# Windowed attention, forward and backward: one 64x64-mode stretch for four tiles, the last chunk of a projection in two banks, loads on two queues, and a rearranged start and end

## The chip, the cores and the metric

The kernel runs on one core of a Trainium2 chip. The metric is the device time of one execution in microseconds (us). Every kernel was run three times, plus once under the profiler; medians are over these four runs (over three for the 2076.62 us of the kernel before).

## The reference, cut to what matters

The inputs are an image `x` of 256x256 pixels with C = 384 channels, in bfloat16, the weights `wqkv` (384x1152) and `wo` (384x384), and `grad_out`, shaped like `x`. The image is cut into 8x8 windows of 64 tokens, and each window is one attention problem with one head.

```python
qkv = xw @ wqkv                       # xw: windows x 64 tokens x 384
p = softmax(einsum('bqc,bkc->bqk', q, k) * C ** -0.5)
o = einsum('bqk,bkc->bqc', p, v) @ wo
# outputs: o, and the gradients of x, wqkv and wo for grad_out
```

There are 1024 windows. The kernels put two windows on the 128 partitions (a "tile") and handle four tiles (a "quad", n = 0 to 127) in a step.

## The kernel before: the parts that matter

The weights are multiplied with each other once at the start (`A` = the scaled product of the q and k weights, `B` = that of the v weights and `wo`, and both transposes). The loop is a software pipeline: step n finishes quad T = n, does the scores and the softmax of S = n + 1, and the projections of A = n + 2.

PSUM is `PS`, eight banks of 512 float32 a partition. `PB` holds the softmax's probabilities and their gradient, `YHT` the projected x and grad_out (transposed), `YH` the same turned back by a transposing DMA, `TT` the transposed `PB`, `MD` what the output and the gradient of x are made from, and `VW` what the weight gradients are made from. The parts that the change touches:

```python
def load(n):                                     # eight loads, one queue (SyncE, "SP")
    for t in range(4):
        SP.dma_start(out=X[:, (n % NX) * 4 + t, :], in_=img(x, n, t))
        SP.dma_start(out=DO[:, (n % ND) * 4 + t, :], in_=img(grad_out, n, t))

def proj(n, a, banks, engs):                     # three chunks of 512 columns, a bank each
    ...
    for mo in range(CK):
        o = PS[:, banks[mo], :]
        for m in range(CK):
            mm(o.rearrange("p (t k) -> p t k", t=4), wgt[:, m, mo * P:(mo + 1) * P], src[:, m, :, :],
               m == 0, m == CK - 1)
        ev(engs[mo], YHT[:, n % NYH, a, mo, :], o)

# the order of a step (conditions cut)
load(n + 4); turn_in(n + 3)                      # loads; transposing DMAs X -> XT, DO -> DOT
scores(S); chain1(S)                             # 64-column products; the softmax's first part on DVE
md(T)                                            # 64x64 products
wgrad(g, k0)
chain2(S); chain3(S)                             # the rest of the softmax: ACT, DVE, POOL
outs(T, 0, 0, ACT); outs(T, 2, 2, DVE); outs_st(T)
proj(A, 0, (4, 5, 0), (ACT, DVE, ACT)); turn_yh(A, 0)
wgrad(g, k0 + 1)
attn(T, 0, 2, 4); attn_ev(T, 0, 2, DVE)          # first stretch in 64x64 mode: two tiles
attn(T, 1, 0, 5); attn_ev(T, 1, 0, ACT)
dxs(T, 0, 4, ACT); dxs_st(T, 0)
proj(A, 1, (2, 3, 1), (DVE, ACT, DVE)); turn_yh(A, 1)
turn_p(S); turn_p_ev(S)                          # transposes of PB, into TT
attn(T, 2, 2, 4); attn_ev(T, 2, 2, ACT)          # second stretch: two tiles
attn(T, 3, 0, 5); attn_ev(T, 3, 0, DVE)
dxs(T, 2, 4, ACT); dxs_st(T, 2)
```

`wgrad` sums a part of a weight gradient over three quads in bank 7, always that bank, and DVE adds it to `ACC`. The plain loads of the weights come first at the start, then `load(0)`, then the transposes of the weights from on-chip memory, all on SP's queue but for the load of `wo`.

Of the kernel before, what the change touches and what calls it, by code (L numbers as in the profile page):

```python
# [9 lines left out]
ALU = mybir.AluOpType  # L10
# [6 lines left out]
def kernel(  # L17
# [27 lines left out]
    PS = pp.tile([P, 8, 512], F32, name="PS")  # L45
    X = sb.tile([P, NX * 4, C], BF16, name="X")
# [42 lines left out]
    def load(n):  # L89
        for t in range(4):  # L90
            SP.dma_start(out=X[:, (n % NX) * 4 + t, :], in_=img(x, n, t))  # L91
            SP.dma_start(out=DO[:, (n % ND) * 4 + t, :], in_=img(grad_out, n, t))  # L92

    def turn_in(n):
        xs = X[:, (n % NX) * 4:(n % NX) * 4 + 4, :].rearrange("p t c -> p (t c)")
        SP.dma_start_transpose(out=XT[:, n % NXT, :, :], in_=xs)  # L96
        ds = DO[:, (n % ND) * 4:(n % ND) * 4 + 4, :].rearrange("p t c -> p (t c)")
        SP.dma_start_transpose(out=DOT[:, n % NDT, :, :], in_=ds)  # L98
# [5 lines left out]
    def proj(n, a, banks, engs):  # L104
        wgt = A_sb if a == 0 else BT_sb
        src = (XT[:, n % NXT] if a == 0 else DOT[:, n % NDT]).rearrange("p (t m) k -> p m t k", m=CK)
        for mo in range(CK):
            o = PS[:, banks[mo], :]
            for m in range(CK):
                mm(o.rearrange("p (t k) -> p t k", t=4), wgt[:, m, mo * P:(mo + 1) * P], src[:, m, :, :],  # L110
                   m == 0, m == CK - 1)
            ev(engs[mo], YHT[:, n % NYH, a, mo, :], o)
# [18 lines left out]
    def chain2(n):  # L131
        ACT.activation(out=PEX[:], in_=SS[:], func=ACTF.Exp)
# [11 lines left out]
    def turn_p(n):  # L144
        bb = PS[:, 6, :].bitcast(BF16)
        for t in range(4):
            for a in range(2):
                for w in range(2):
                    r = slice(64 * w, 64 * w + 64)
                    PE.transpose(bb[r, t * P + a * 64:t * P + a * 64 + 64], PB[r, n % 2, a, t, :], ident[r, r])  # L150

    def turn_p_ev(n):
        ev(DVE, TT[:, n % 2].rearrange("p t a k -> p (t a k)"), PS[:, 6, :].bitcast(BF16)[:, 0:512])

    def md(n):
        for m in range(CK):
# [22 lines left out]
    def attn(n, t, bvw, bdx):  # L179
        xs, ds, vw = (n % NX) * 4 + t, (n % ND) * 4 + t, (n % NVW) * 4 + t  # L180
        for a in range(2):
            src = X[:, xs, :] if a == 0 else DO[:, ds, :]
            yh = YH[:, n % NTOK, a, :, :].rearrange("p (m t) k -> p t m k", m=CK)[:, t]
            for cr in range(2):
                for w in range(2):
                    r = slice(64 * w, 64 * w + 64)
                    o = 64 * (w if cr == 0 else 1 - w)
                    if cr == 0:
                        mm(PS[o:o + 64, bvw + a, 0:C], PB[r, n % 2, a, t, :], src[r, :], True, True)
                    else:  # L190
                        mm(PS[o:o + 64, bdx, 0:C].rearrange("p (m k) -> p m k", m=CK), PB[r, n % 2, a, t, :],
                           yh[r], a == 0, False)

    def attn_ev(n, t, bvw, eng):
        ev(eng, VW[:, (n % NVW) * 4 + t, :, :], PS[:, bvw:bvw + 2, 0:C])

    def dxs(n, t0, b0, eng):
        for i in range(2):
            for m in range(CK):
                mm(PS[:, b0 + i, 0:C], MD[:, m, t0 + i, 0:2, :].rearrange("p a k -> p (a k)"), AT_sb[:, m, :],  # L200
                   False, m == CK - 1)
        ev(eng, DXS[:, n % 2, t0:t0 + 2, :], PS[:, b0:b0 + 2, 0:C])
# [6 lines left out]
    def wgrad(g, k):  # L209
        quads = range(g * GQ, min(NQ, (g + 1) * GQ))  # L210
        which, ma = k // CK, k % CK
        tiles = [(q, t) for q in quads for t in range(4)]
        for i, (q, t) in enumerate(tiles):
            mm(PS[:, 7, 0:C], X[:, (q % NX) * 4 + t, ma * P:(ma + 1) * P], VW[:, (q % NVW) * 4 + t, which, :],
               i == 0, i == len(tiles) - 1)
        if g == 0:
            DVE.tensor_copy(out=ACC[:, k, :], in_=PS[:, 7, 0:C])
        else:
            DVE.tensor_tensor(out=ACC[:, k, :], in0=PS[:, 7, 0:C], in1=ACC[:, k, :], op=ALU.add)  # L219

    with tc.manual_schedule():

        wT = VW[:].rearrange("p a b c -> p (a b c)")[:, 0:JK * C].rearrange("p (j c) -> p j c", j=JK)
        wo_sb = VW[:].rearrange("p a b c -> p (a b c)")[:, JK * C:(JK + CK) * C].rearrange("p (m c) -> p m c", m=CK)
        for m in range(CK):
            SP.dma_start(out=w_sb[:, m, :], in_=wqkv[m * P:(m + 1) * P, :])
        ACT.dma_start(out=wo_sb[:], in_=wo.rearrange("(m p) n -> p m n", p=P))
        make_identity(nc, ident[:])
        load(0)
        for m in range(CK):  # L230
            SP.dma_start_transpose(out=wT[:, :, m * P:(m + 1) * P], in_=w_sb[:, m, :])  # L231
        for m in range(CK):
            SP.dma_start_transpose(out=woT_sb[:, :, m * P:(m + 1) * P], in_=wo_sb[:, m, :])  # L233
        k = 0
        for dst, lt, r0, sc in ((A_sb, wT[:, 0:CK], wT[:, CK:2 * CK], True),
                                (AT_sb, wT[:, CK:2 * CK], wT[:, 0:CK], True),
                                (B_sb, wT[:, 2 * CK:3 * CK], wo_sb, False),
                                (BT_sb, wo_sb, wT[:, 2 * CK:3 * CK], False)):
            for mo in range(CK):
                o = PS[:, k % 8, 0:C]  # L240
                for m in range(CK):
                    mm(o, lt[:, m, mo * P:(mo + 1) * P], r0[:, m, :], m == 0, m == CK - 1)
                if sc:
                    ACT.activation(out=dst[:, mo, :], in_=o, func=ACTF.Copy, scale=scale)
                else:
                    DVE.tensor_copy(out=dst[:, mo, :], in_=o)
                k += 1

        def step(n):
            T, S, A = n, n + 1, n + 2  # L250
            doT, doS, doA = 0 <= T < NQ, 0 <= S < NQ, 0 <= A < NQ
            g, k0 = n // GQ - 1, 2 * (n % GQ)
            doF = 0 <= g < NG
            if 0 < n + 4 < NQ:
                load(n + 4)
            if 0 <= n + 3 < NQ:
                turn_in(n + 3)
            if doS:
                scores(S)
                chain1(S)  # L260
            if doT:
                md(T)
            if doF:
                wgrad(g, k0)
            if doS:
                chain2(S)
                chain3(S)
            if doT:
                outs(T, 0, 0, ACT)
                outs(T, 2, 2, DVE)  # L270
                outs_st(T)
            if doA:
                proj(A, 0, (4, 5, 0), (ACT, DVE, ACT))
                turn_yh(A, 0)
            if doF:
                wgrad(g, k0 + 1)
            if doT:
                attn(T, 0, 2, 4)
                attn_ev(T, 0, 2, DVE)
                attn(T, 1, 0, 5)  # L280
                attn_ev(T, 1, 0, ACT)
                dxs(T, 0, 4, ACT)
                dxs_st(T, 0)
            if doA:
                proj(A, 1, (2, 3, 1), (DVE, ACT, DVE))
                turn_yh(A, 1)
            if doS:
                turn_p(S)
                turn_p_ev(S)
            if doT:  # L290
                attn(T, 2, 2, 4)
                attn_ev(T, 2, 2, ACT)
                attn(T, 3, 0, 5)
                attn_ev(T, 3, 0, DVE)
                dxs(T, 2, 4, ACT)
                dxs_st(T, 2)

        for n in range(-3, GQ * NG + GQ):
            step(n)


        GF = YHT[:, 0].rearrange("p a m t -> p (a m t)")[:, 0:6 * C].rearrange("p (k c) -> p k c", k=6)
        GFT = YHT[:, 1].rearrange("p a m t -> p (a m t)")[:, 0:6 * C].rearrange("p (k c) -> p k c", k=6)
        for k in range(6):
            ev(DVE if k < 3 else ACT, GF[:, k, :], ACC[:, k, :])
        for h in range(2):
            for mb in range(CK):
# [3 lines left out]
                ev(DVE if h == 0 else ACT, GFT[:, h * CK + mb, :], pt[:, 0:C])  # L311
        dw = VW[:].rearrange("p a b c -> p (a b c)")[:, 0:CK * J].rearrange("p (m j) -> p m j", m=CK)
        dwo = VW[:].rearrange("p a b c -> p (a b c)")[:, CK * J:CK * J + CK * C].rearrange("p (m j) -> p m j", m=CK)
        k = 0
        for ma in range(CK):
            for col, lt, rr, r0 in ((0, GF[:, 0:CK], w_sb, C), (C, GFT[:, 0:CK], w_sb, 0), (2 * C, GFT[:, CK:], woT_sb, 0)):
# [46 lines left out]
```

## Time and profile before

The time before is 2076.62 us (median of three runs, 2074.34 to 2076.63). These lines are from the first, third and fourth parts of its profile page: busy time, share of the span and number of instructions by engine (PE is the matmuls of TensorE, PEld its weight loads); the two large DMA queues with packets, MB and the share of 16 engines' time (q1 is what SyncE issues, q0 what GpSimd issues; ScalarE's few loads are on q10, under 1 MB); and the chain of waits that ended last, by engine.

```profile
PE 2029.9 (98%) x26970; PEld 1149.4 (55%) x26970; DVE 1358.6 (66%) x2452; ACT 985.1 (48%) x1555; POOL 1012.9 (49%) x1798
q1 hardware_dynamic: 956304, 305.37, 84.1%
q0 software_dynamic: 73728, 101.02, 18.2%
PE 96%; DMA 2%; SPq 2%; DVE 0%; ACT 0%; issue 0%; DVEq 0%
```

TensorE is the limit. I take a step as the time from the first score product of one quad to that of the next. The windows view of the kernel before, cut at the scores of quad 1, quad 6 and quad 127, shows the three stages: head, 121 full steps and tail. Columns: stretch, its length, busy us (and instructions) of PE, PEld, DVE, ACT and POOL, the granted clock, the DMA share (the summed time of all packets over that of 16 engines, so it can pass 1), GB/s.

```profile
0.00:42.55 42.55, 21.48 (x137) 9.89 (x138) 10.19 (x20) 8.15 (x14) 2.03 (x8) 0.92 0.81 176
42.55:122.32 79.77, 70.59 (x979) 37.80 (x978) 50.21 (x89) 37.30 (x59) 37.45 (x66) 0.98 1.01 200
122.32:2017.68 1895.36, 1894.67 (x25412) 1076.88 (x25411) 1274.46 (x2299) 921.97 (x1452) 956.70 (x1694) 1.00 1.06 203
2017.68:2072.70 55.02, 43.20 (x447) 24.80 (x446) 23.71 (x44) 17.63 (x30) 16.72 (x30) 0.98 0.24 62
```

In the third line PE is busy 1894.67 of 1895.36 us: a gain there has to come out of PE's own order of work. But "busy" hides short stalls, since the ends of matmuls are modelled. The timeline of the kernel before, at the second attention stretch of one step, shows such a stall (columns: start, duration, engine, line, operation, out<-in, number, and in brackets the idle time before it):

```profile
1013.08 0.69 DVE L79 CAST YHT<-PS 128x512 bf16<-128x512 f32 x1 [0.67 <-PE PS L73]
...
1013.35 0.33 PE L73 MATMUL PS<-DO,PB 64*64 64x384 bf16 x2
1013.45 0.33 PE L73 MATMUL PS<-YH,PB 64*64 64x384 bf16 x2
1013.51 0.33 PE L73 MATMUL PS<-X,PB 64*64 64x384 bf16 x2
...
1013.83 0.35 PE L73 MATMUL PS<-DO,PB 64*64 64x384 bf16 x2
```

Pairs of matmuls on one tile start every 0.16 us (1013.35 to 1013.51), but the next pair starts 0.32 us later, at 1013.83. DVE's eviction of the projection's last chunk, which holds bank 1, ended at 1013.77; the stalled products write bank 1. The stall is 0.155 us by the unrounded starts, in every step.

Waits of PE outside the steady state, from the waits view of the kernel before (us in total, times, longest):

```profile
PE PS L73 <- DMA VW<-w_sb: 14.0, 1, 14.0
PE PS L73 <- DMA XT<-X: 10.2, 5, 3.5
PE PS L73 <- DVE ACC L219: 4.5, 7, 0.6
```

They are the start (the transposed weights), the first steps (the transposed x) and the end (bank 7 shared by the last weight gradients).

### The profile page before, as it was taken

To read this page: it belongs to the slowest core of one execution; us is meant where nothing else is said; L and a number is where in the kernel's file an instruction comes from. 1 tells how busy PE (TensorE), PEld (TensorE's weight loads), DVE (VectorE), ACT (ScalarE), POOL (GpSimd) and SP (SyncE) were. 2 spreads that over 40 slices of the span, in tenths; PEclk is the share of its full clock that TensorE was granted. 3 is DMA by queue.
4 is the path that set the end of the run, shared out by engine and by line. 5 is a ranking of instruction groups with operands and counts; after the bars stand their busy time and mean duration, and the time that the engine had idled before them with its cause. 6 is when DMAs were issued, how large, how long until landed. Compare 5 with 4: busy or idle time off the path is not lost.

```text
span 2072.7 us, 65934 instructions
## 1 busy us (share of the span) xinstructions
PE 2029.9 (98%) x26970; PEld 1149.4 (55%) x26970; DVE 1358.6 (66%) x2452; ACT 985.1 (48%) x1555; POOL 1012.9 (49%) x1798
## 2 busy tenths in 40 slices
PE   5899999999999999999999999999999999999997
PEld 2455555555555555555555555555555555555554
DVE  3566666666666666666666666666666666666664
ACT  2444444444445444444444444544444444444452
POOL 1454555555555455455555555545545555555552
PEclk9999999999999999999999999999999999999999
DMA  8999999999999999999999999999999999999991
GB/s 177 203 202 202 208 201 197 209 205 198 205 207 200 204 206 200 202 209 198 206 200 205 203 204 203 202 203 205 200 201 208 202 201 204 206 204 200 206 177 56
DMA packets 1030734, 410.90 MB, mean 198 GB/s; under 512 B 865056, under 2 KB 1013280, under 8 KB 1030432
## 3 DMA queue, kind: packets, MB, share of 16 engines
q1 hardware_dynamic: 956304, 305.37, 84.1%
q0 software_dynamic: 73728, 101.02, 18.2%
q8 instruction: 212, 3.47, 0.7%
q14 instruction: 90, 0.74, 0.1%
q10 hardware_dynamic: 400, 0.29, 0.0%
HBM read 101.84 MB, written 101.84 MB: 98 GB/s over the span
## 4 chain that ended last, share of the span: by engine, by line
PE 96%; DMA 2%; SPq 2%; DVE 0%; ACT 0%; issue 0%; DVEq 0%
PE PS L73 94%; PE PS L150 2%; DMA XT<-X 1%; SPq L92 0%; SPq L91 0%; SPq L231 0%; DMA VW<-in_wo_dram 0%; DVE ACC L219 0%; SPq L233 0%; ACT DXS L77 0%; ACT YHT L77 0%; SPq L98 0%; DVE YHT L79 0%; SPq L96 0%; PE PS L310 0%
## 5 line engine op out<-in xcount | busy, mean ns | idle before, releaser
L207 POOL DMA_DIRECT2D out_dram<-DXS x1024 | 572.8, 566 | 583.7 <-ACT DXS L77 561.4
L73 PE MATMUL PS<-VW,X 128*128 128x384 bf16 x3072 | 542.7, 326 | 4.5 <-DVE ACC L219 4.5
L73 PEld LDWEIGHTS <-X 64*64 64x64 bf16 (+1 forms) x9216 | 380.3, 104 | 218.8 <-issue 6.9
L79 DVE CAST YHT<-PS 128x512 bf16<-128x512 f32 x384 | 264.3, 688 | 240.4 <-PE PS L73 238.4
L73 PEld LDWEIGHTS <-MD 128*128 128x128 bf16 x3072 | 279.3, 98 | 232.4 <-issue 61.5
L77 ACT CAST VW<-PS 128x768 bf16<-128x768 f32 x256 | 204.3, 798 | 367.6 <-PE PS L73 367.6
L77 ACT CAST YHT<-PS 128x512 bf16<-128x512 f32 x384 | 224.7, 585 | 277.6 <-PE PS L73 253.7
L219 DVE TENSOR_TENSOR ACC<-PS,ACC 128x384 f32<-128x384 f32 x252 | 140.5, 558 | 257.3 <-PE PS L73 257.3
L73 PE MATMUL PS<-AT_sb,MD 128*128 128x384 bf16 x1536 | 294.1, 328 | 0.0
L141 POOL TENSOR_TENSOR UM<-PB,ST 128x256 f32<-128x256 bf16 x128 | 77.8, 608 | 424.1 <-PE PS L73 367.8
L73 PE MATMUL PS<-XT,A_sb 128*128 128x512 bf16 x1152 | 273.7, 383 | 10.4 <-DMA XT<-X 10.2
L177 POOL DMA_DIRECT2D out_dram<-OS x512 | 276.1, 545 | 13.9 <-issue 11.4
L73 PE MATMUL PS<-B_sb,MD 128*128 128x384 bf16 x1536 | 271.5, 326 | 4.3 <-DVE MD L79 2.5
L73 PE MATMUL PS<-DOT,BT_sb 128*128 128x512 bf16 x1152 | 270.5, 380 | 0.0
L77 ACT CAST DXS<-PS 128x768 bf16<-128x768 f32 x256 | 204.3, 798 | 138.3 <-PE PS L73 138.3
L79 DVE CAST VW<-PS 128x768 bf16<-128x768 f32 x256 | 244.0, 953 | 18.6 <-PE PS L73 4.8
L79 DVE CAST MD<-PS 128x512 bf16<-128x512 f32 x384 | 240.2, 681 | 0.6 <-PE PS L73 0.6
L73 PE MATMUL PS<-YH,PB 64*64 64x384 bf16 x2048 | 238.6, 332 | 1.0 <-ACT DXS L77 1.0
L77 ACT CAST MD<-PS 128x512 bf16<-128x512 f32 x384 | 200.1, 594 | 67.1 <-DVE ST L128 64.6
L77 ACT CAST OS<-PS 128x768 bf16<-128x768 f32 x128 | 102.1, 798 | 194.5 <-PE PS L73 194.5
L73 PEld LDWEIGHTS <-A_sb 128*128 128x128 bf16 x1152 | 113.4, 99 | 135.6 <-issue 12.4
L73 PEld LDWEIGHTS <-BT_sb 128*128 128x128 bf16 x1152 | 113.1, 98 | 123.8 <-issue 2.4
(46 smaller groups left out, 1618.6 us busy)
## 6 DMA issues: line engine op xcount, KB each, us to landing
X<-in_x_dram SPq DMA_DIRECT2D x512, 96.0 KB, 3.1
DO<-in_grad_out_dram SPq DMA_DIRECT2D x512, 96.0 KB, 3.2
out_dram<-OS POOLq DMA_DIRECT2D x512, 96.0 KB, 2.9
out_dram<-DXS POOLq DMA_DIRECT2D x1024, 48.0 KB, 3.8
YH<-YHT SPq DMA_TRANSPOSE x256, 5.4
XT<-X SPq DMA_TRANSPOSE x128, 6.6
DOT<-DO SPq DMA_TRANSPOSE x128, 6.5
w_sb<-in_wqkv_dram SPq DMA_DIRECT2D x3, 288.0 KB, 4.0
```

The lines of the kernel that those rows point to most:

```text
L73: PE.matmul(out, lhsT=lhsT, rhs=rhs, start=start, stop=stop, skip_group_check=True)
L77: ACT.copy(out=out, in_=in_)
L79: DVE.tensor_copy(out=out, in_=in_)
L141: POOL.tensor_tensor(out=UM[:], in0=pb[:, 1], in1=bcast(3), op=ALU.mult)
L150: PE.transpose(bb[r, t * P + a * 64:t * P + a * 64 + 64], PB[r, n % 2, a, t, :], ident[r, r])
L177: POOL.dma_start(out=img(out_0, n, t), in_=OS[:, n % 2, t, :])
L207: POOL.dma_start(out=img(out_1, n, t)[8 * w:8 * w + 8], in_=DXS[64 * (1 - w):64 * (1 - w) + 64, n % 2, t, :])
L219: DVE.tensor_tensor(out=ACC[:, k, :], in0=PS[:, 7, 0:C], in1=ACC[:, k, :], op=ALU.add)
```

## The change

Its intent, as I read the diff: (1) the four attention products of a step stand together, so that the engine enters and leaves the 64x64 mode once where it did twice; PSUM is addressed flat, and products that cross a bank are cut at its edge; the softmax's first part moves behind `md`. (2) The last chunk of each projection goes to two banks in halves, so that two engines evict it in halves. (3) The loads of x move from SP's queue to POOL's. (4) At the start, the weights are transposed straight from memory, the loads are spread over three queues and held back by small POOL copies ("gates"), and the first projections start earlier. (5) At the end, the last eight weight gradients use five banks, and the last products are reordered.

```diff
-    def load(n):
+    def load_x(q, n):
         for t in range(4):
-            SP.dma_start(out=X[:, (n % NX) * 4 + t, :], in_=img(x, n, t))
-            SP.dma_start(out=DO[:, (n % ND) * 4 + t, :], in_=img(grad_out, n, t))
+            q.dma_start(out=X[:, (n % NX) * 4 + t, :], in_=img(x, n, t))
+    def load_do(q, n):                            # the same for grad_out
 ... in proj:
-            o = PS[:, banks[mo], :]
+            for t0, t1 in ((0, 4),) if mo < CK - 1 else ((0, 2), (2, 4)):
+                o = PS[:, banks[i], 0:P * (t1 - t0)]
 ... 
+    def attn_all(n, S):
+        v = (n % NVW) * 4
+        fvw = ((3072, 3584), (1536, 1920), (2304, 2688), (3072, 3584))   # columns; a bank has 512
+        for t in range(4):
+            attn(n, t, 0, fvw[t][0], t * C)
+            if t == 2:
+                ev(ACT, VW[:, v + 1, :, :].rearrange("p a c -> p (a c)"), PSF[:, 1536:2304])
+            attn(n, t, 1, fvw[t][1], t * C)
+            if t == 0:
+                ev(ACT, VW[:, v, 0, :], PSF[:, 3072:3456])
+                ev(DVE, VW[:, v, 1, :], PSF[:, 3584:3968])
+        ev(DVE, VW[:, v + 2, :, :].rearrange("p a c -> p (a c)"), PSF[:, 2304:3072])
+        if S is not None:
+            turn_p(S)
+        ev(ACT, VW[:, v + 3, 0, :], PSF[:, 3072:3456])
+        ev(DVE, VW[:, v + 3, 1, :], PSF[:, 3584:3968])
+        if S is not None:
+            turn_p_ev(S)
 ... the new order of a step (conditions cut)
+        load_do(SP, n + 4); load_x(POOL, n + 4); turn_in(n + 3, 0); turn_in(n + 3, 1)
+        scores(S); md(T); chain1(S)
+        wgrad(g, k0)
+        chain2(S); chain3(S)
+        outs(T, 0, 0, ACT); outs(T, 2, 2, DVE); outs_st(T)
+        wgrad(g, k0 + 1)
+        proj(A, 0, (3, 1, 2, 5), (ACT, DVE, ACT, DVE)); turn_yh(A, 0)
+        attn_all(T, S if doS else None)
+        dxs(T, 0); dxs_ev(T, 0, ACT)
+        proj(A, 1, (3, 4, 5, 7), (ACT, DVE, ACT, DVE)); turn_yh(A, 1)
+        dxs(T, 1); dxs_ev(T, 1, ACT)
 ... the start (cut)
         for m in range(CK):
-            SP.dma_start(out=w_sb[:, m, :], in_=wqkv[m * P:(m + 1) * P, :])
+            SP.dma_start_transpose(out=wT[:, 0:2 * CK, m * P:(m + 1) * P], in_=wqkv[m * P:(m + 1) * P, 0:2 * C])
+        load_x(ACT, 0)
+        load_do(POOL, 0)
+        for i in range(14):
+            mm(PS[:, 7, :], wsrc[:, 0:P], wsrc, True, True)
+        wprod(A_sb, wT[:, 0:CK], wT[:, CK:2 * CK], True)
+        gate(A_sb[0:1, 2, 0:1])                   # a POOL copy: POOL's later loads wait for it
 ... the end (cut)
+        for n in range(NQ, GQ * NG + GQ):
+            for i in range(2):
+                wgrad(n // GQ - 1, 2 * (n % GQ) + i, (3, 4, 5, 6, 7)[b % 5])
+                b += 1
```

## The prediction

> **What bounds it now.** TensorE. The page's first part has PE busy 98%; the windows view has it busy 156.60 of 156.60 us anywhere in the middle; the chain of waits is 96% PE. The timeline shows equal steps (four 8x8-window tiles each): score products start every 15.66 us. DVE 66%, ACT 48%, POOL 49% are not the limit.
>
> One step, by PE starts in the timeline: scores 0.88, md 0.79, weight gradient 1.96, outs 1.95, projection 1.95, weight gradient 2.04, attention of two tiles 0.78, dx 0.98, projection 2.04, transposes and attention of two tiles 1.21, dx 1.08 us. Four 64x64 matmuls already run side by side (one group of four per 0.163 us), so the attention products alone need 1.30 us.
>
> **What changes in a step.**
> - Merging two 64x64 stretches removes two changes of tile mode. The Trainium skill, "TensorEngine Tiling (Array Packing)", Key Properties, says that a change of mode drains the engine; the trace agrees: a projection or attention group followed by another mode is 0.09 to 0.13 us longer. Gain about 0.21 us.
> - The second stretch stalls 0.155 us before the last tile, waiting for DVE's 0.69 us eviction of the projection's last chunk. Two half evictions and later use remove it.
> - Split matmuls cost little: 128-column transposes follow each other every 0.056 us, so a cut adds about 3 ns; about 16 cuts on the critical path, 0.06 us.
> - New: the softmax's first part now stands behind DVE's three MD evictions (0.63 us each). By my sum DVE ends the output eviction of bank 3 about 7.7 us into the step; the projection that now starts with bank 3 is ready at 7.53. I expect a stall of 0 to 0.25 us there.
>
> Net 0.08 to 0.28 us a step; I take 0.17, times 121 full steps: 20 us.
>
> **Head.** Before, the first five steps take 11.7, 14.3, 15.6, 18.2 and 16.1 us, though three of them lack weight gradients (about 11.6 us of PE work); PE waits there for the XT transposes (waits view), and the SP queue issues without a pause: eight loads of about 0.64 us and four transposes of 2.1 to 2.6 us. Moving x loads to POOL takes 2.5 us a step from SP; transposing weights straight from memory shortens the start. Scores of step 0 should move from 42.6 to about 27 us, and step 5 from 122.3 to about 100: 20 us (12 to 28).
>
> **Tail.** The last eight weight gradients share one bank: six 0.65 us waits for DVE in the timeline, and more elsewhere. Five banks remove them: about 5 us. No separate cast of the gradients, fewer stalls in the last step, reordered outputs: about 4 us. In all 9 us.
>
> **Off the path.** POOL gets four more DMA issues a step (0.56 us each): about 10.3 of 15.5 us, still ahead of the transposes of P. DMA bytes do not change. In steady state SP is already ahead of PE, so its relief buys nothing there.
>
> **Sum:** 2076.6 - 20 - 20 - 9 = about 2027 us. Range 1998 to 2050. Chances: faster by over 2% 0.66, within 2% 0.32, slower 0.02.
>
> **What would show it.** Timeline: step period 15.4 to 15.58; one attention stretch near 1.3 us followed without a gap by the transposes; PE waits for the DVE output eviction before the first projection, if my stall is real; scores of step 0 near 27 us; tail from the last step's end to the span's end about 23 us, before 31.
>
> **What would make it wrong.** Bank conflicts between attention groups and evictions in the tightly packed banks (t=3 needs banks 6 and 7 about 0.1 us after they come free); POOL's late x loads delaying XT; SWDGE loads slowing the transposes; head loads serialized by the gates.

## The result, and the profile after

The kernel after is correct. Its time is 2020.70 us (median of four runs, 2020.39 to 2021.47), beside 2076.62 us of before. The ratio is 0.9734, with a 95% interval of 0.9717 to 0.9751. Ratios here are those of the runs of the two kernels in the same rounds, so not quite the ratio of the medians that I quote.

The page of the kernel after, the same parts as before:

```profile
PE 1987.0 (98%) x30568; PEld 1321.4 (65%) x30568; DVE 1392.1 (69%) x2705; ACT 1014.3 (50%) x1810; POOL 1287.7 (64%) x2312
q1 hardware_dynamic: 882128, 254.31, 78.2%
q0 software_dynamic: 98304, 151.39, 28.7%
PE 95%; DMA 2%; issue 1%; SPq 1%; ACT 0%; DVE 0%; POOL 0%; ACTq 0%; POOLq 0%; DVEq 0%
```

The limit is still TensorE, and some 50 MB of loads have moved from q1 to q0. The windows view of the kernel after, cut at the same events (scores of quads 1, 6 and 127):

```profile
0.00:37.02 37.02, 24.58 (x162) 12.06 (x163) 10.72 (x23) 8.55 (x17) 12.95 (x30) 0.86 0.90 167
37.02:113.52 76.50, 67.06 (x1119) 45.01 (x1119) 50.38 (x99) 38.16 (x69) 45.41 (x82) 0.98 1.17 214
113.52:1970.89 1857.37, 1853.89 (x28800) 1238.08 (x28800) 1308.39 (x2541) 950.46 (x1694) 1212.07 (x2171) 1.00 1.10 207
1970.89:2019.69 48.80, 41.51 (x491) 26.24 (x490) 22.64 (x42) 17.16 (x30) 17.25 (x31) 1.00 0.29 73
```

Subtracting stage by stage gives where the 53.0 us between the two profiled spans came from:

| stage | before | after | gain | predicted |
|---|---|---|---|---|
| head, to the scores of quad 6 ("step 5") | 122.32 | 113.52 | 8.8 | 20 |
| 121 full steps | 1895.36 (15.664 each) | 1857.37 (15.350 each) | 38.0 | 20 |
| tail, from the last scores | 55.02 | 48.80 | 6.2 | 9 |

The sum came out as predicted to within 4 us (49 against 53.0), but from other parts: the steady steps gave twice what I had expected, the head less than half.

The median step fell from 15.658 to 15.311 us, below the 15.4 to 15.58 that the prediction names. (The mean of after, 15.350, is higher because of six slow steps, up to 16.89 us.) The pieces of one step, measured between the starts of their first matmuls (us; a piece that ends in a stall or in a change of mode holds it):

| piece | before | after |
|---|---|---|
| scores, md | 0.88 + 0.80 | 0.88 + 0.80 |
| two weight gradients | 1.961 + 2.044 | 1.961 + 1.966 |
| outs | 1.950 | 1.950 |
| two projections | 1.942 + 2.036 | 2.041 + 1.950 |
| attention and the transposes of PB | 0.776 + 1.209 | 1.334 + 0.366 |
| dx, two halves | 0.986 + 1.078 | 0.993 + 1.076 |

A 128x128 group that is followed by attention is 0.08 to 0.09 us longer (2.044 against 1.961, 2.041 against 1.950). Before there were two such groups in a step, after there is one. The attention and transposes together fell from 1.985 to 1.700 us.

The timeline of the kernel after around the first projection and the attention. The bank-3 wait that I had predicted shows in its first two lines: DVE's eviction ends at 12.40 and the projection starts at 12.45.

```profile
1011.45 0.95 DVE L80 CAST OS<-PS 128x768 bf16<-128x768 f32 x1
1012.45 2.11 PE L74 MATMUL PS<-XT,A_sb 128*128 128x512 bf16 x12
...
1014.49 0.35 PE L74 MATMUL PS<-X,PB 64*64 64x384 bf16 x2
...
1015.50 0.33 PE L74 MATMUL PS<-X,PB 64*64 64x384 bf16 x2
...
1015.66 0.34 PE L74 MATMUL PS<-DO,PB 64*64 64x384 bf16 x2
...
1015.82 0.43 PE L157 MATMUL PS<-ident,PB 64*64 64x64 bf16 x16
```

The projection starts 0.05 us after DVE is done, so it does wait for DVE. But by the unrounded starts it follows the last matmul of the weight gradient after 0.178 us, where the pitch of such matmuls is 0.163; the wait costs about 0.015 us. The attention runs from 1014.49 to 1015.82 in one piece, and the transposes follow without a gap.

PE's waits in the kernel after:

```profile
PE PS L74 <- DMA XT<-X: 7.5, 2, 5.3
PE PS L74 <- DMA VW<-in_wqkv_dram: 7.1, 1, 7.1
PE PS L74 <- DVE ACC L255: 0.7, 2, 0.4
```

The wait for the weights looks halved, but that is because the 14 added matmuls on zeros keep PE busy for 5.58 us first: the first product of the weights starts at 13.83 us, where it was 13.97. (Five later runs whose start issues the same DMAs have it at 12.89 to 13.14 us; see the caution under "The head".)

### The profile page after: what moved, and what is told of

It reads as the page before. It is cut to its first block, busy times and chain, and to the rows that moved or that the text cites. A ratio compares the mean times of both kernels' runs of the same rounds, so it can differ in the third digit from the quotient of the medians.

```text
span 2019.7 us, 73659 instructions
## 1 busy us (share of the span) xinstructions
PE 1987.0 (98%) x30568; PEld 1321.4 (65%) x30568; DVE 1392.1 (69%) x2705; ACT 1014.3 (50%) x1810; POOL 1287.7 (64%) x2312
## 3 DMA queue, kind: packets, MB, share of 16 engines
q0 software_dynamic: 98304, 151.39, 28.7%
## 4 chain that ended last, share of the span: by engine, by line
PE 95%; DMA 2%; issue 1%; SPq 1%; ACT 0%; DVE 0%; POOL 0%; ACTq 0%; POOLq 0%; DVEq 0%
PE PS L74 94%; PE PS L157 2%; DMA X<-in_x_dram 1%; DMA out_dram<-DXS 1%; DMA XT<-X 0%; DMA out_dram<-OS 0%; SPq L340 0%; SPq L96 0%; ACT DXS L78 0%; SPq L100 0%; ACT VW L379 0%; SPq L92 0%; DMA DO<-in_grad_out_dram 0%; DVE OS L80 0%; POOL out_dram L243 0%
## 5 line engine op out<-in xcount | busy, mean ns | idle before, releaser
L78 ACT CAST YHT<-PS 128x512 bf16<-128x512 f32 (+1 forms) x512 | 246.0, 480 | 451.5 <-PE PS L74 445.9
L80 DVE CAST YHT<-PS 128x512 bf16<-128x512 f32 (+1 forms) x512 | 269.5, 556 | 206.3 <-PE PS L74 206.2
L80 DVE CAST VW<-PS 128x384 bf16<-128x384 f32 (+1 forms) x384 | 253.3, 687 | 95.8 <-ACT VW L78 92.1
L92 POOL DMA_DIRECT2D X<-in_x_dram x504 | 270.3, 553 | 45.1 <-DMA out_dram<-DXS 30.3
L74 PE MATMUL PS<-AT_sb,MD 128*128 128x384 bf16 (+2 forms) x2304 | 294.7, 273 | 1.8 <-ACT DXS L78 1.8
L74 PE MATMUL PS<-XT,A_sb 128*128 128x512 bf16 (+1 forms) x1536 | 273.1, 328 | 7.6 <-DMA XT<-X 7.5
L74 PE MATMUL PS<-DOT,BT_sb 128*128 128x512 bf16 (+1 forms) x1536 | 270.8, 326 | 0.6 <-DVE YHT L80 0.5
L78 ACT CAST VW<-PS 128x384 bf16<-128x384 f32 (+1 forms) x384 | 212.5, 587 | 58.1 <-PE PS L74 42.7
L74 PE MATMUL PS<-YH,PB 64*64 64x256 bf16 (+2 forms) x3072 | 195.2, 273 | 0.0
L74 PE MATMUL PS<-X,PB 64*64 64x384 bf16 (+2 forms) x1536 | 170.6, 273 | 4.2 <-DVE OS L80 2.4
```

The costliest lines, as they stand in the source:

```text
L74: PE.matmul(out, lhsT=lhsT, rhs=rhs, start=start, stop=stop, skip_group_check=True)
L78: ACT.copy(out=out, in_=in_)
L80: DVE.tensor_copy(out=out, in_=in_)
L92: q.dma_start(out=X[:, (n % NX) * 4 + t, :], in_=img(x, n, t))
```

## The experiments

Theory after the result: the steady gain is the sum of the stall removed and the mode changes saved, and, as I had predicted, the move of the x loads has no part in it. Rivals: the second queue is what allows the shorter step; the halves do more than remove the one stall; the single stretch is worth more, or less, than its mode changes. For the head: the order of the queues, the gates, the way the weights arrive, or the DMA engines themselves hold it back.

| run | what | us, median (range) | ratio to before, interval | median / mean step |
|---|---|---|---|---|
| before (first session) | | 2076.62 (2074.34 to 2076.75) | | 15.658 / 15.664 |
| after | | 2020.70 (2020.39 to 2021.47) | 0.9734, 0.9717 to 0.9751 | 15.311 / 15.350 |
| a_two | after, attention in two stretches | 2074.62 (2073.33 to 2076.08) | 0.9992, 0.9978 to 1.0007 | 15.744 / 15.767 |
| a_two2 | the same, other banks | 2068.89 (2065.91 to 2071.28) | 0.9963, 0.9946 to 0.9979 | 15.700 / 15.731 |
| a_one | after, last chunks whole | 2032.15 (2030.47 to 2032.84) | 0.9786, 0.9770 to 0.9803 | 15.417 / 15.425 |
| a_spx | after, x loads on SP | 2103.10 (2101.08 to 2106.49) | 1.0131, 1.0116 to 1.0146 | 15.879 / 16.040 |
| a_spi | the same, loads interleaved | 2105.46 (2102.30 to 2107.19) | 1.0138, 1.0123 to 1.0153 | 15.844 / 16.023 |
| b_half | before, second projection in halves | 2060.83 (2058.14 to 2063.35) | 0.9926, 0.9911 to 0.9940 | 15.480 / 15.561 |
| b_halfsplit | b_half, x loads on POOL | 2053.29 (2052.79 to 2053.81) | 0.9888, 0.9873 to 0.9903 | 15.480 / 15.484 |
| b_tail | before, five banks at the end | 2069.67 (2068.77 to 2070.23) | 0.9967, 0.9952 to 0.9982 | 15.658 / 15.667 |
| a_wplain | after, weights loaded plain first | 2018.38 (2017.42 to 2020.56) | 0.9722, 0.9708 to 0.9737 | 15.312 / 15.323 |
| a_headq | after, first grad_out loads on ACT | 2022.76 (2021.06 to 2023.04) | 0.9740, 0.9726 to 0.9755 | 15.312 / 15.331 |
| a_nogate | after, no gates | 2021.81 (2019.30 to 2025.66) | 0.9743, 0.9727 to 0.9760 | 15.312 / 15.321 |
| a_best | a_wplain, transposes before loads | 2018.00 (2015.02 to 2019.67) | 0.9717, 0.9702 to 0.9731 | 15.308 / 15.333 |

The before of the three sets of experiments had medians of 2075.21, 2076.45 and 2076.67 us. All kernels gave the right result. Steps are those of one profiled execution each, the 121 from the scores of quad 6 on.

### The halves alone, in the kernel before (b_half, b_halfsplit)

```diff
 in proj
-        o = PS[:, banks[mo], :]
+        for t0, t1 in ((0, 4),) if mo < CK - 1 or a == 0 else ((0, 2), (2, 4)):
+            o = PS[:, banks[i], 0:P * (t1 - t0)]
 in step
-                proj(A, 1, (2, 3, 1), (DVE, ACT, DVE))
+                proj(A, 1, (2, 3, 0, 1), (DVE, ACT, DVE, ACT))
```

> The kernel before, with only the second projection's last chunk cut into two halves in two banks, evicted by DVE and ACT. Theory (the 0.155 us stall before the last tile's products is the wait for that eviction): the stall goes, period 15.66 -> about 15.5 us, time 2076.6 -> about 2057 us. Rival (halving alone is not enough, the later use of the banks removed it): time within 5 us of 2076.6, a wait of over 0.1 us still before the last tile's products.

b_half took 2060.83 us. Its median step is 15.480, 0.178 less than before: the stall is gone, and the size is that of the stall with a little more. But its mean step is 0.081 above its median, and one wait has grown. In the waits view of b_half:

```profile
PE PS L73 <- DMA XT<-X: 19.5, 14, 4.0
```

It was 10.2 us in 5 times in the kernel before. The transposed x comes late now and then, so something on its way had been just fast enough for 15.66 us. b_halfsplit puts the x loads of quads 8 and later on POOL's queue and leaves all else:

```diff
-            SP.dma_start(out=X[:, (n % NX) * 4 + t, :], in_=img(x, n, t))
+            (SP if n < 8 else POOL).dma_start(out=X[:, (n % NX) * 4 + t, :], in_=img(x, n, t))
```

> b_half (the kernel before with the second projection's last chunk in two banks) plus the x loads on the second queue from quad 8 on. Theory: b_half's mean step was 0.08 us over its median because the one load queue had begun to bind; with two queues TensorE's waits for the transposed x (19.5 us in b_half) go, the mean step falls from 15.56 to 15.48 us and the time is about 2051 us (2047 to 2055). Rival: the slow steps have another cause (contention of the DMA engines, which the second queue does not lessen), and the time stays at 2060 us, within 3.

It took 2053.29 us. The mean step fell to 15.484, next to the median of 15.480. In the waits view of b_halfsplit:

```profile
PE PS L73 <- DMA XT<-X: 12.9, 6, 3.9
```

All of it lies in the first 115 us, so the waits of the steady state are gone (b_half had 5.9 us of its 19.5 after that point). The theory holds, a little short in size (2051 expected). So halves and second queue together are worth 0.180 us a step on the mean, and the halves alone only 0.103.

### The second queue, in the kernel after (a_spx, a_spi)

```diff
-            load_x(POOL, n + 4)
+            load_x(POOL if n < 8 else SP, n + 4)
```

> The changed kernel, but x loads go back to the SP queue from the fourth quad pair on (head as in the changed kernel). Theory of the prediction (the relief of SP buys nothing in the middle): period stays 15.31, time within 4 us of 2020.7. Rival (the SP queue needed about 15.7 us a step before, issuing without a pause, so it would bind below that): period 15.5 to 15.8 us, PE waits for XT in the middle, time 2040 to 2075 us.

a_spx took 2103.10 us, 82 us more than after and more than before; even the rival had said 2040 to 2075. The claim of my prediction that SP's relief "buys nothing" is wrong. The waits view of a_spx:

```profile
PEld L74 <- DMA XT<-X: 106.6, 100, 2.6
PE PS L74 <- DMA XT<-X: 75.5, 68, 5.9
```

Of its 121 steps 34 stay below 15.4 us, as in after; the others take up to 17.5 us, and one 19.3. In a_spx all x loads of a step stand behind all grad_out loads; the kernel before interleaves them. a_spi interleaves them as before does:

```diff
+            else:
+                for t in range(4):
+                    SP.dma_start(out=X[:, ((n + 4) % NX) * 4 + t, :], in_=img(x, n + 4, t))
+                    SP.dma_start(out=DO[:, ((n + 4) % ND) * 4 + t, :], in_=img(grad_out, n + 4, t))
```

> The kernel after with all its loads on SyncE's queue, as in a_spx, but with the x and the grad_out loads of a step interleaved as the kernel before has them. Theory A (order): a_spx was so slow because its x loads all stood behind the grad_out loads; interleaved, the queue only just binds, the mean step is 15.5 to 15.6 us and the time about 2050 us. Theory B (one queue is too slow for this order of work, whatever the order of the loads): the mean step stays at 16.0 us and the time at about 2100 us.

a_spi took 2105.46 us, the same as a_spx: theory B, and the order of the loads is not it. The chain of waits of a_spi in time order, a cut from the middle (start, us, what), shows the path through SP's queue and the transpose:

```profile
1026.63 0.60 SPq L287
...
1027.32 0.55 SPq L288
1027.86 0.05 issue
1027.92 5.29 DMA XT<-X
1033.20 0.05 issue
1033.25 3.58 PE PS L74 x60
```

How full the queue is can be summed from the trace between 300 and 1900 us. SP's DMA issues take 1502 us of these 1600 in before, 1504 in b_half, 1505 in a_spx and 1503 in a_spi, and pauses over 0.3 us sum to under 6 us in each. In after they take 1299 us and the pauses sum to 228; in b_halfsplit 1346 and 180. An issue has no fixed length (the first two transposes of x in before took 1.62 and 1.70 us to issue, those of the steady state 2.15 on the mean), so these sums alone would not show a limit. With the two pairs of runs that differ in nothing but the queue (a_spx and after, b_half and b_halfsplit) they do: one queue of twelve DMAs a step is about as slow as TensorE was before, and slower than TensorE is after.

The Trainium skill, page "Trainium Kernel Development and Optimization", section Key Constraints, says of DMAs issued from several engines that this "only saves the sequencer's issue time". The bytes moved are the same, 410.9 MB in before and 411.4 in after, so no traffic was saved; whether all of it shares the DMA engines no run here tests. But to take the x loads off SP's queue was worth 4% of the kernel.

What stays open: b_half manages a mean of 15.56 us with one queue, a_spx and a_spi only 16.0, with the same twelve DMAs. The order of x and grad_out is excluded. The new moments at which the `YH` transposes and the stores come are left, and I did not try them. Nor is it shown what holds the queue. The moved loads change the issuing engine and the DMA queue (q1 to q0) together, and with the x loads gone a grad_out load takes 0.81 us on the mean to issue in after, where it took 0.58 in before. So part of an issue may be waiting for something behind the queue. The x loads on ScalarE's queue would be a test; it was not run.

### The halves, in the kernel after (a_one)

```diff
-            for t0, t1 in ((0, 4),) if mo < CK - 1 else ((0, 2), (2, 4)):
+            for t0, t1 in ((0, 4),):
```

> The changed kernel, but the last chunk of each projection whole in one bank, evicted by ACT. If the halves matter in the new order: ACT ends the first projection's last eviction 0.2 us later and the fourth tile's products wait for bank 6, period 15.31 -> 15.4 to 15.5 us, time 2035 to 2045 us. If the new order alone removed the stall: period within 0.03 us of 15.31, time within 4 us of 2020.7.

It took 2032.15 us, a little below the expected 2035 to 2045, with a median step of 15.417 as expected, 0.106 more than after. The pieces show that the attention is 1.449 us long instead of 1.334. The timeline of a_one, PE and then ACT:

```profile
1004.59 0.22 PE L74 MATMUL PS<-YH,PB 64*64 64x128 bf16 x2
1004.75 0.35 PE L74 MATMUL PS<-X,PB 64*64 64x384 bf16 x2
```

```profile
1003.73 0.59 ACT L78 CAST YHT<-PS 128x512 bf16<-128x512 f32 x1 [0.71 <-PE PS L74]
1004.22 1.69 ACT L78 CAST VW<-PS 128x384 bf16<-128x384 f32 x3
```

The jump from 1004.59 to 1004.75 is ahead of the fourth tile, which writes the banks that the first tile's `VW` evictions hold. ACT comes to its one only after the whole last chunk of the projection (0.59 us; in after it has a half of 0.37 us there). So the halves are needed in the new order too, in another place: this is the tight spot at banks 6 and 7 that the prediction named as a danger. The same run measures a cut: the projections with 9 uncut matmuls take 2.032 and 1.942 us, with 12 they take 2.041 and 1.950, so each of the three additional matmuls costs about 0.003 us. The Trainium skill, "TensorE: Matmul & The Clock Gate", section "Wait — 56ns, not 53.3ns?", gives about 2.5 ns as a fixed cost of a matmul.

### One stretch or two (a_two, a_two2)

```diff
-        for t in range(4):
+        for t in ((0, 1) if half == 0 else (2, 3)):
 in step
-            attn_all(T, S if doS else None)
+            attn_all(T, S if doS else None, 0)
             dxs(T, 0); dxs_ev(T, 0, ACT)
-            proj(A, 1, (3, 4, 5, 7), (ACT, DVE, ACT, DVE))
+            proj(A, 1, (4, 5, 3, 7), (ACT, DVE, ACT, DVE))
+            attn_all(T, S if doS else None, 1)
             dxs(T, 1); dxs_ev(T, 1, ACT)
```

> The changed kernel, but with the attention products in two stretches of two tiles again (the second with the transposes of P), the second projection between them as before; same matmuls, same loads. Theory (two changes of tile mode removed are worth about 0.21 us a step): step period 15.31 -> about 15.5 us, time 2020.7 -> about 2047 us. Rival (the gain came from the removed stall or from the evictions' order, not from the number of tile-mode changes): period within 0.04 us of 15.31, time within 5 us of 2020.7.

It took 2074.62 us: both numbers were missed, and by its ratio it is no faster than before. Its step is 0.43 us longer than that of after. About 0.2 of it are the mode changes; the rest are two waits that my arrangement of banks had made, some 0.09 us at bank 5 and 0.15 ahead of the scores. a_two2 changes banks and engines to remove them:

```diff
-                proj(A, 1, (4, 5, 3, 7), (ACT, DVE, ACT, DVE))
+                proj(A, 1, (4, 5, 3, 7), (ACT, ACT, DVE, ACT))
 and the eviction of TT goes ahead of those of the fourth tile's VW
```

> The kernel after with the attention products in two stretches of two tiles again, this time with the banks and eviction engines of the projections arranged so that no bank is waited for at the second stretch (in a_two 0.09 us at bank 5 and about 0.15 us at bank 6 were waits I had made myself). Theory: one stretch saved costs only two mode changes, 0.19 us of TensorE a step, so the median step is about 15.50 us (15.31 + 0.19) and the time about 2045 us (2038 to 2052). Rival: the two stretches cost more than the mode changes, the step stays at 15.7 us or above and the time at 2070 us or above.

It took 2068.89 us with a median step of 15.700, so my 15.50 was missed again and the rival's number was met. The pieces of a_two2 against after say why: the projection before the second attention is +0.094 us, the two attentions together +0.139 (0.782 + 0.691 against 1.334), and 0.15 are again waits of my own arrangement. One is before the scores (+0.086), where ACT evicts bank 6 late. The other is a longer weight gradient before the first projection (2.031 against 1.966):

```profile
1080.74 0.95 DVE L80 CAST OS<-PS 128x768 bf16<-128x768 f32 x1
1081.74 0.59 PE L74 MATMUL PS<-XT,A_sb 128*128 128x512 bf16 x2
```

This is the bank-3 wait that I had predicted for after: DVE ends at 1081.69, a little later than it would in after, and the projection starts at 1081.74. So the wait is real, and in after all but some hundredths of a microsecond of it are avoided. These two runs give 0.23 us (0.094 + 0.139) as the cost of the second stretch without the other waits. They are no clean measure of it, as other banks were moved too. A second reading comes from b_halfsplit, whose two stretches have the original banks and no stall: its median step is 0.169 us above that of after. By pieces that is 0.07 at the second weight gradient and the two projections (6.028 against 5.956 together: two of the three stand ahead of a stretch there, one in after), and 0.10 at attention and transposes (1.801 against 1.700).

### The head (a_wplain, a_headq, a_nogate, a_best)

In the kernel after, the chain of waits up to the scores of quad 1, 37.02 us, holds 18.0 us of DMAs on their way and 10.4 us of SP's queue, by the sum of its pieces. In the kernel before it was 9.9 us of DMAs and 28.7 us of SP's queue, of 42.55. A cut of the chain in after (start, us, what):

```profile
3.15 8.32 DMA X<-in_x_dram
...
11.55 1.42 SPq L100
...
13.02 1.57 SPq L340
...
21.12 3.39 DMA X<-in_x_dram
24.52 6.31 DMA XT<-X
30.84 0.04 issue
30.88 1.47 PE PS L74 x6
```

From 11.55 to 21.12 us it runs through SP's queue, which had to wait for quad 0's x and then issued transposes and loads one after the other. The last of quad 0's four x loads is issued at 3.15 us and lands 8.32 us later; the median of x loads on the page is 4.3 us. The three transposes of the weights from memory are issued from 0.74 to 3.50 us and land at 5.49, 10.27 and 13.69 us. I tried three ways around this, and a fourth in the last set. a_wplain loads the weights plain and transposes them on chip:

```diff
-            SP.dma_start_transpose(out=wT[:, 0:2 * CK, m * P:(m + 1) * P], in_=wqkv[m * P:(m + 1) * P, 0:2 * C])
+            SP.dma_start(out=w_sb[:, m, :], in_=wqkv[m * P:(m + 1) * P, :])
+        for m in range(CK):
+            SP.dma_start_transpose(out=wT[:, 0:2 * CK, m * P:(m + 1) * P], in_=w_sb[:, m, 0:2 * C])
```

> The changed kernel, but the weights are loaded plainly first and transposed from SBUF, as in the kernel before (the late reload of wqkv falls away). Theory (transposes straight from memory took 10.2 us to land and cost the head what the shorter path was to bring): first weight product at 10 to 11.5 us instead of 13.8, scores of step 0 at 34 to 36 instead of 37.0, time about 2017 us. Rival (DMA traffic of the head as a whole sets it): first product within 1 us of 13.8, time within 2 us of 2020.7.

The first weight product starts at 12.67 us instead of 13.83, the scores of quad 1 at 34.28 instead of 37.02, those of quad 6 at 112.78 instead of 113.52. The first product missed its 10 to 11.5, and beside the spread of one and the same start (12.89 to 13.83, 34.05 to 37.02 and 112.52 to 117.38 us, see below) none of the three stands out by more than 0.2 us. The time, 2018.38 us, can't be told from after: the intervals of the two ratios overlap.

a_headq puts the grad_out loads of the first steps on ScalarE's queue, a_nogate drops the gates:

```diff
 a_headq
-            load_do(SP, n + 4)
+            load_do(ACT if n < 1 else SP, n + 4)
 a_nogate
-        gate(A_sb[0:1, 2, 0:1])
-        gate(BT_sb[0:1, 2, 0:1])
```

> The changed kernel, but grad_out loads of the first three steps issue from the ACT queue. Theory (in the head SP's in-order queue delays the XT transpose: PE waited 5.3 us for it at 44 us): that wait shrinks to under 1 us, time about 2016 us. Rival (the DMA engines are the limit in the head): wait stays over 4 us, time within 2 us of 2020.7.

> The changed kernel without the two gates on POOL in the head, so that the loads behind them issue at about 4 us. If gating protects the weights' transposes: first product later than 13.8 us, time up by 1 to 4 us. If not: later loads land earlier, time down by 1 to 4 us or unchanged.

a_headq took 2022.76 us, with the scores of quad 6 at 117.42 and a longest wait for the transposed x of 7.5 us, so not under 1; a_nogate took 2021.81, with the first weight product at 15.47 instead of 13.83 and the scores of quad 6 at 114.89. Neither is faster. The gates seem to do what they are for, since without them the first product comes 1.6 us later than in after, and later than in any profiled run with them (12.89 to 13.83 us with this start), but the end result is the same.

a_best adds to a_wplain the order "transposes before loads" in the first steps:

```diff
+        if 1 < n + 4 < NQ and n < 1:              # after turn_in, instead of before it
+            load_do(SP, n + 4)
+            load_x(POOL, n + 4)
```

> a_wplain (weights loaded plain and transposed on chip) and, in the first step, the transposing loads issued ahead of the plain ones. Theory: the wait for the transposed x near 43 us (6.9 us in a_wplain) shrinks to about 4.5 us and the time is 2015 to 2018 us. Rival: the DMA engines bound the start, so the order of issues only moves the wait elsewhere, and the time is within 2 us of 2018.4.

The longest wait was 4.5 us, as expected, and 6.9 in a_wplain; but runs with an unchanged start differ by as much (below). The waits view of a_best within its first 115 us:

```profile
PE PS L74 <- DMA XT<-X: 5.8, 2, 4.5
```

The time is 2018.00 us (2015.02 to 2019.67), which fits both expectations and decides nothing. It is the lowest median; I don't call it better than after, as the intervals of the ratios overlap.

A caution belongs to all four. The profiled runs of a_two, a_two2, a_one, a_spx and a_spi issue the DMAs of the start as after does. Yet their first weight product starts at 12.89 to 13.14 us where after has 13.83, their scores of quad 1 at 34.05 to 35.02 (37.02 in after), those of quad 6 at 112.52 to 117.38 (113.52), and their longest wait for the transposed x at the start is 5.9 to 8.1 us (5.3). So one look at the head is uncertain by some microseconds, and effects of 1 to 3 us there were not to be settled with these runs. What they do show is that no rearrangement brought the scores of quad 1 below 34 us, far from the 27 that I had predicted.

### The tail (b_tail)

```diff
-            mm(PS[:, 7, 0:C], ...
+            mm(PS[:, bank, 0:C], ...                # bank = (3, 4, 5, 6, 7)[b % 5] for the last eight
```

> The kernel before, with only the last eight weight gradients spread over five PSUM banks. Theory: the waits of 0.65 us between them go, tail (from the last scores to the end) 55.0 -> about 50 us, time about 2071.5 us. Rival: DVE's additions set the pace, tail within 1 us of 55.

It took 2069.67 us, and its tail is 49.35 us instead of 55.02: 5.7 us from the banks alone. In the timeline of the kernel before, the pattern that this removes:

```profile
2047.32 1.46 PE L73 MATMUL PS<-VW,X 128*128 128x384 bf16 x8 [0.65 <-DVE ACC L219]
2049.42 1.46 PE L73 MATMUL PS<-VW,X 128*128 128x384 bf16 x8 [0.65 <-DVE ACC L219]
```

The whole tail of after gains 6.2 us, so everything else that the change does at the end is worth about 0.5.

## Why the prediction was right or wrong, point by point

The total was right: 2027 us predicted, 2020.70 measured, inside the range, and faster by over 2% as given the highest chance. That it came so close is partly luck, because errors cancelled: the steady state gave 18 us more than I had said, the head and the tail 14 less.

**What bounds the kernel: right.** TensorE, before and after; 98% busy in both.

**The steady state: right in its mechanisms, too small in size.** I predicted 0.17 us a step and 20 us; it was 0.314 us on the mean (0.347 on the median) and 38.0 us. The terms on the median:

| term | predicted | measured |
|---|---|---|
| stall at the second stretch | +0.155 | +0.178 (b_half) |
| mode changes | +0.21 | about +0.2 (worked out below) |
| cuts | -0.06 | about -0.03 |
| bank-3 wait | 0 to -0.25 | about -0.015 |

The last three together are measured, as the 0.169 us between b_halfsplit and after. Cuts cost about 0.017 in the projections (a_one), half of which b_halfsplit has too, and by the pieces some 0.01 to 0.02 more in the attention and the dx products; with the bank-3 wait that leaves 0.20 to 0.21 for the mode changes. That is an estimate from these differences and not a measurement by itself. The Trainium skill's statement that a change of mode drains the engine ("TensorEngine Tiling (Array Packing)", Key Properties) agrees with the 0.08 to 0.09 us by which a group ahead of the attention is longer.

The mis-sized term was the bank-3 wait. I took half of "0 to 0.25" off the gain. My sum had DVE free 7.7 us into the step, and it was free after 7.51 (1012.40 less the step's start at 1004.89). a_two2 shows how near it was: there DVE is free 0.06 us later, and the projection is held back by 0.08 us.

**"In steady state SP is already ahead of PE, so its relief buys nothing there": wrong.** This is the step of the prediction that failed. SP's queue was ahead only of a TensorE that needed 15.66 us a step. In the kernel before the transposed x was issued some 18 us ahead of the scores that use it, and I took that as slack; but the queue issued without a pause all the while, which I had seen and used for the head only. Nor are the scores its first user. The first projection is: it starts 7.79 us after the issue, and the transpose lands 6.65 us after it (medians of 100 steps). So the trace before had 1.0 us to spare, and 0.27 at the least; in after it is 11.7. a_spx shows what the step is without the relief, 16.04 us. Without the second queue the whole change would have been a loss of 1.3%. The error didn't show in the total, as the change had the relief in it.

**The head: right in direction, wrong in size.** I predicted the scores of quad 1 near 27 us and those of quad 6 near 100; they came at 37.02 and 113.52, a gain of 8.8 us instead of 20 (one profile each). SP's queue was indeed most of the old path, 28.7 of 42.55 us. The step that failed was to take nearly all of its relief as gain: in after 10.4 us of it remain, and the DMAs' time on their way grew from 9.9 to 18.0 us. The transposes straight from memory were no large shortcut either (first weight product 12.89 to 13.83 us with this start, 13.97 before). A check that I could have made: 37.02 us at 167 GB/s are 6.2 MB moved by the scores of quad 1, part of them for later quads. To move them in 27 us takes 229 GB/s. The busiest of the 40 slices of 50 us on the page of after has 225, and from 125 to 152 us it moves 239, so 229 would be near the most that this kernel ever moved. That the DMA engines are the head's limit is a guess from this and from the landing times; no run shows it.

**The tail: the banks right, the rest too high.** Five banks gave 5.7 us (predicted 5), everything else about 0.5 (predicted 4), together 6.2 instead of 9.

**Off the path: right.** POOL is busy 1212.07 us in 121 steps, 10.0 us a step (predicted 10.3), and holds up nothing. The DMA bytes did not change.

**The named dangers.** The tight banks 6 and 7 are real but are just avoided by the halves (a_one). Late x loads by POOL don't show: after the head, the waits view of after has no wait for XT. The transposes did not get slower (the pages have the transposed x landing 6.2 us after its issue, 6.6 before). The gates cost nothing that could be measured.

## What to carry to other kernels

When a stage is shortened, ask of every other resource whether it keeps up with the new period, not the old one: a queue that issues without a pause (here 1502 of 1600 us) has little slack, whatever lead it shows, and the slack is read from the landing to the first use (here 1.0 us). To take load off such a queue may gain little by itself (no run here tries it alone) and still be what makes another gain possible (here 82 us). Evictions that stand ahead of others on an engine decide bank waits on TensorE by hundredths of a microsecond; to cut the last one in halves on two engines removed 0.18 us a step before and 0.11 after. A start that is rearranged to issue DMAs sooner is only shorter if the bytes can also arrive sooner; to divide the MB to be moved by the GB/s that the profile shows is a first check, not a proof.

## What the Trainium skill lacked or had wrong

- Page "Trainium Kernel Development and Optimization", section Key Constraints: that issuing from several engines "only saves the sequencer's issue time" has no size beside it. The same DMAs with the x loads on a second queue took 2020.70 us instead of 2103.10, and 2053.29 instead of 2060.83; whether all of that is issue time stays open here. That a queue busy with issuing can be the limit is not missing from the skill as a whole. On no page that I read did I find a measured length of an issue in a loaded steady state on this chip; here it was on the mean 0.58 to 0.67 us for a 96 KB load and 2.1 to 2.7 us for a transpose in the kernel before, against 1.6 to 1.9 us for the first two transposes each of x and of grad_out.
- Page "TensorEngine Tiling (Array Packing)", Key Properties: the drain at a change of mode is named without a size. Here a group of matmuls that is followed by a 64x64 stretch is 0.08 to 0.09 us longer, and a second stretch in a step costs 0.17 us (b_halfsplit against after) to 0.23 us (a_two2).
- Page "TensorE: Matmul & The Clock Gate": nothing wrong; its fixed cost of about 2.5 ns a matmul is what three additional matmuls cost here (0.0085 us, 2.8 ns each).
